# The first transfer ahead of the opening barrier, and the closing barrier with semaphores alone, in a single-core decode kernel

## The chip, the cores and the metric

The program runs on one core of one Trainium2 chip. The metric is the device time of one execution in microseconds (us). "Span" is the time from the first to the last instruction of the program in a profile; mostly about 2 us of each execution lie outside the span. Engines: PE is TensorE (PEld its weight loads), DVE is VectorE, ACT is ScalarE, POOL is GpSimd, SP is SyncE; a q after the name is the engine's sequencer. A timed run also gives its span, without a trace; a trace is one execution.

## The reference

```python
x = A_x                                            # 1 x 1 x 512, bf16
h = x + attention(layernorm(x), k_cache, v_cache, wq, wo)   # 32 query heads, 8 kv heads, 65536 keys of 128
h2 = h + ((sigmoid(g) * u) @ w_down)               # g, u: layernorm(h) @ w_gate, @ w_up; 512 -> 1792 -> 512
```

One token is decoded. The two caches are 134 MB each and are read once; the weights are 13.9 MB. There is little arithmetic per byte.

## The kernel before

Python records operations per engine and emits them with semaphores. SyncE issues every large transfer; they go to four ring slots of 4 MB.

```python
order = [("wq", 0)]                                # then K0, K1, K2, K3, K4, V0, K5, V1, ...
order += [("K", b) for b in range(NR)]
# ... cut ...
order += [("V", NB - 4), ("V", NB - 3), ("V", NB - 2), ("V", NB - 1), ("wg", 0), ("wu", 0), ("wd", 0)]
dma("act", lambda e: e.dma_start(x_row[:, :], A_x[0]), "x", name="x")
# ... cut: SyncE's transfers, each waiting until its ring slot is free; then the arithmetic ...
dma("sp", lambda e: e.dma_start(out[0].rearrange("o (g n) -> (o g) n", g=4), ...), "out", ["ysb"], "out")
op("sp", lambda e: None, ["out"])                  # SyncE waits for the output
block = es.enter_context(nc.Block("main"))         # opens one body per engine, closes with a barrier
P.emit(block)
```

The built program begins and ends with a barrier of all five engines. Each engine drains and increments a gather semaphore; GpSimd waits until it is 4, then increments a release semaphore, on which the others wait (in the trace of the opening one the gathers come at 0.01 to 0.34 us, SyncE's release at 0.66). GpSimd writes four constants before the opening one. SyncE's instructions, as built (wait in brackets):

```
opening: Drain [release == 0, then gather += 1]; EventSemaphore [release >= 1]; branch to SyncE's body
body:    DMACopy wq; DMACopy K0, K1, K2; ...; DMACopy out [y copied]; branch [output landed]
closing: Drain [release == 0, then gather += 1]; EventSemaphore [release >= 1]
```

Of the kernel before, what the change touches and what calls it, by code (L numbers as in the profile page):

```python
# [32 lines left out]
HINTED = ("pe", "dve", "act")  # L33


class Prog:
# [3 lines left out]
    def __init__(self, nc, es):  # L40
        self.nc, self.es = nc, es
        self.ops = {e: [] for e in ("pe", "act", "dve", "pool", "sp")}
        self.where = {}
        self.alias = {}
        self.dma_sems = {}
        self.loop_sems = {}
        self.flow = {}
        self.part = {}

    def op(self, eng, fn, deps=(), name=None, to=None, times=1):  # L50
        assert name is None or name not in self.where, name
        self.ops[eng].append(dict(fn=fn, deps=[d for d in deps if d], name=name, dma=None, to=to, times=times, part=self.part.get(eng)))
        if name:
            self.where[name] = (eng, len(self.ops[eng]) - 1)
# [4 lines left out]
        rec["count"] += 16  # L59
        self.ops[eng][-1]["dma"] = (sem, rec["count"])  # L60

    def emit(self, block):
        for ops in self.ops.values():
            for o in ops:
                o["deps"] = [self.alias.get(d, d) for d in o["deps"]]
        needed = {d for ops in self.ops.values() for o in ops for d in o["deps"]}
        sems = {e: self.es.enter_context(self.nc.semaphore(f"s_{e}")) for e in self.ops}
        for k, rec in self.dma_sems.items():
            rec["sem"] = self.es.enter_context(self.nc.semaphore(f"d_{k}"))
        extra = {k: self.es.enter_context(self.nc.semaphore(f"p_{k}"))  # L70
                 for k in sorted({o["to"] for ops in self.ops.values() for o in ops if o["to"]})}
        parts = {}
        for e in self.flow:
            byname = {}
            for o in self.ops[e]:
                if o["part"]:
                    byname.setdefault(o["part"][0], {}).setdefault(o["part"][1], []).append(o)
            parts[e] = byname
            for inst in byname.values():
                for same in zip(*inst.values(), strict=True):  # L80
                    assert len({o["to"] for o in same}) == 1
                    if any(o["name"] in needed for o in same):
                        for o in same:
                            o["inc"] = True
        value = {}
        counts = {}
        for e, ops in self.ops.items():
            n = 0
            for o in ops:
                if o["dma"]:  # L90
                    k, v = o["dma"]
                    value[o["name"]] = (self.dma_sems[k]["sem"], v, k)
                elif o["to"]:
                    k = o["to"]
                    counts[k] = counts.get(k, 0) + 1
                    if o["name"]:
                        value[o["name"]] = (extra[k], counts[k], k)
                    o["inc"] = True
                elif o["name"] in needed or o.get("inc"):
                    n += o["times"]  # L100
                    value[o["name"] or id(o)] = (sems[e], n, e)
                    o["inc"] = True

        def waits_of(e, o, seen, off, loop):
            want = {}
            for d in o["deps"]:
                sem, v, key = value[d]
                own = self.loop_sems.get(key, (None,))[0]
                assert own in (None, e) and not (loop and own is None), (o["name"], d)
                v -= off.get(key, 0)  # L110
                if v > seen.get(key, 0) and v > want.get(key, (None, 0))[1]:
                    want[key] = (sem, v)
            for key, (sem, v) in want.items():
                seen[key] = v
            return list(want.values())

        def put(e, eng, o, waits):
            for sem, v in waits:
                eng.wait_ge(sem, v)
            ins = o["fn"](eng)  # L120
            if o["dma"]:
                ins.then_inc(self.dma_sems[o["dma"][0]]["sem"], 16)
            elif o["to"]:
                ins.then_inc(extra[o["to"]], 1)
            elif o.get("inc"):
                ins.then_inc(sems[e], 1)

        def run(e, eng):
            ops = self.ops[e]
            if e not in self.flow:  # L130
                seen = {}
                for o in ops:
                    put(e, eng, o, waits_of(e, o, seen, {}, False))
                return
            at = [i for i, o in enumerate(ops) if o["part"]]
            head, tail = ops[:at[0]], ops[at[-1] + 1:]
            assert at == list(range(at[0], at[-1] + 1))
            seen = {}
            for o in head:
                put(e, eng, o, waits_of(e, o, seen, {}, False))  # L140
            off, plan, took, seq = {}, {}, {}, []
            for o in ops[at[0]:at[-1] + 1]:
                if not seq or seq[-1] != o["part"]:
                    seq.append(o["part"])
            assert len(set(seq)) == len(seq)
            for p, r in seq:
                s2 = {}
                w = [waits_of(e, o, s2, off, len(parts[e][p]) > 1) for o in parts[e][p][r]]
                assert plan.setdefault(p, w) == w, (p, r, plan[p], w)
                for k, v in s2.items():  # L150
                    took[k] = max(took.get(k, 0), v)
                for k, (own, down) in self.loop_sems.items():
                    if own == e and p in down:
                        assert took[k] >= down[p], (k, p, r)
                        took[k] -= down[p]
                        off[k] = off.get(k, 0) + down[p]

            done = set()

            def section(p):  # L160
                assert p not in done
                done.add(p)
                inst = list(parts[e][p].values())[-1]
                for o, w in zip(inst, plan[p]):
                    put(e, eng, o, w)
                for k, (own, down) in self.loop_sems.items():
                    if own == e and p in down:
                        eng.sem_inc(extra[k] if k in extra else self.dma_sems[k]["sem"], -down[p])

            self.flow[e](eng, section)  # L170
            assert done == set(parts[e])
            seen = {k: v for k, v in seen.items() if k not in self.loop_sems}
            for o in tail:
                put(e, eng, o, waits_of(e, o, seen, off, False))

        def hinted(e, eng):

            if self.ops[e][0]["dma"]:
                put(e, eng, self.ops[e].pop(0), [])
            here = OrderedEngineSet([eng.engine])  # L180
            never = self.nc.alloc_registers(f"never_{e}", engines=here)
            first, end = f"first_{e}", f"end_{e}"
            self.nc.regs_mov(never, 1)
            self.nc.br(first, engines=here)
            with self.nc.body(first, valid_engines=here):
                loc = eng.mark_branch_hint_location()
                run(e, eng)
                eng.br_lt(never, 1, on_true=first, on_false=end).branch_hint(loc)
            self.nc.switch_bb(end)

        for e, deco in (("sp", block.sync), ("pool", block.gpsimd), ("act", block.scalar),
                        ("dve", block.vector), ("pe", block.tensor)):
            deco((lambda eng, e=e: hinted(e, eng)) if e in HINTED else (lambda eng, e=e: run(e, eng)))


def bass_sequential_preLN__gqa_block_cached__glu_gated_glu__decode_kernel(
# [18 lines left out]
    with ExitStack() as es:  # L215
# [69 lines left out]
        P = Prog(nc, es)  # L285
        op, dma = P.op, P.dma
# [29 lines left out]
        for ld in order:  # L316
# [3 lines left out]
            deps = [freed(prev[ld])]  # L320
# [103 lines left out]
        regs, R, here = [], {}, OrderedEngineSet([mybir.EngineType.PE])  # L424
# [323 lines left out]
        for i in range(HKV + 1):  # L748
            loop = 0 < i < HKV
            for r in range(NR):  # L750
# [7 lines left out]
                if i:  # L758
                    v = NR * (i - 1) + r
# [32 lines left out]
        for i, (nm, bank) in enumerate((("wg", GB), ("wu", UB))):  # L792
            at = slot_of[(nm, 0)] * SLOT + W_AT[nm]
# [19 lines left out]
        for i, (r0, r1) in enumerate(WD_SPLIT):  # L813
            for r in range(r0, r1):
                for g in range(4):
# [5 lines left out]
        op("dve", lambda e: e.tensor_copy(y_sb[:, :], ps(YB, 0, 128)), ["y"], "ysb")  # L821
        dma("sp", lambda e: e.dma_start(out[0].rearrange("o (g n) -> (o g) n", g=4),
                                        bass.AP(tensor=y_sb, offset=0, ap=[[32 * 128, 4], [1, 128]])), "out", ["ysb"], "out")
        op("sp", lambda e: None, ["out"])

        block = es.enter_context(nc.Block("main"))
        P.emit(block)


# [26 lines left out]
```

## Time and profile before

| | before |
|---|---|
| median of the first 3 runs | 663.49 us |
| span of the profiled run | 660.9 us |
| bytes moved, mean rate | 282.3 MB, 427 GB/s |
| wq issued, first packet (records of the trace) | 0.737, 1.744 us |
| output semaphore full, SyncE's signal to the closing barrier, last release ended | 660.453, 660.643, 660.850 us |

From the page of the kernel before: the span, the busy share of the 16 DMA engines in 40 equal slices (9 is 90% or more), the rate of each slice, and the share of one queue.

```profile
span 660.9 us, 6130 instructions
...
DMA  9999999999999999999999999999999999999997
GB/s 381 440 418 438 434 426 440 420 438 434 424 440 424 434 438 420 440 424 436 436 420 440 432 428 438 420 438 434 426 440 419 438 434 426 440 422 421 435 421 320
...
q1 hardware_dynamic: 11208, 282.33, 99.5%
```

The transfers fill the time; only the first and the last slice are low. So the time is a head before the first byte, a stream, and a tail after it.

The start in the timeline of the kernel before (start, duration, engine, line, operation, what ended the idle time before it):

```profile
0.73 0.51 ACTq L312 DMA_DIRECT2D x_row<-in_A_x_dram  x1
0.74 0.39 SPq L322 DMA_DIRECT2D ring<-in_A_wq_dram  x1
...
1.19 1.46 SPq L345 DMA_DIRECT2D ring<-in_A_k_cache_dram  x3
...
2.04 0.29 PE L402 MATMUL PS<-ident,x_row 1*128 1x1 bf16 x4 [2.04 <-DMA x_row<-in_A_x_dram]
...
7.59 0.30 DVE L408 TENSOR_SCALAR xz<-hT,mo,rstd 128x4 bf16<-128x4 f32 x1 [0.68 <-POOL rstd L396]
...
13.31 0.58 PE L445 MATMUL PS<-qz 128*8 128x512 bf16 x1 [7.17 <-issue]
```

SyncE stands in the barrier for 0.7 us before it issues wq. The normalised x (xz) is ready at 7.9 us, and PE goes on only at 13.3, when wq has landed.

The end, in the same view:

```profile
656.57 0.65 DVE L812 STREAM_TRANSPOSE hhT<-hh 128x448 bf16<-128x448 bf16 x1
...
657.27 1.14 PE L817 MATMUL PS<-ring,hhT 128*1 128x128 bf16 x56 [1.71 <-DVE hhT L812]
658.12 0.10 PEld L817 LDWEIGHTS PS<-ring,hhT 128*1 128x1 bf16 x8 [0.20 <-DMA ring<-in_B_w_down_dram]
658.46 0.29 DVE L821 CAST y_sb<-PS 128x128 bf16<-128x128 f32 x1 [1.24 <-PE PS L817]
658.77 0.66 SPq L822 DMA_DIRECT2D out_dram<-y_sb  x1
```

And SyncE's waits that the change touches (engine and line, for what, total us, times, longest): the branch L215 for the output, the opening barrier L841, the closing barrier L215.

```profile
SPq L215 <- DMA out_dram<-y_sb: 1.0, 1, 1.0
SPq L841 <- PEq L841: 0.7, 1, 0.7
SPq L215 <- PEq L215: 0.2, 1, 0.2
```

### The profile page before, as it was taken

The numbers are of one execution on the slowest core, as the hardware profiler recorded it, in microseconds if no ns is written. First come the engines' busy times: TensorE is split into PE (matmuls) and PEld (weight loads), VectorE is DVE, ScalarE is ACT, GpSimd is POOL, SyncE is SP. The second block draws the span as 40 slices with busy tenths as digits, with TensorE's granted clock in tenths as the row PEclk, the third lists the DMA queues.
The fourth block names the chain that finished last, engine by engine and source line by source line (L and its number), as shares of the span: only waits on it lengthen the run. The fifth ranks groups of instructions, "written<-read, shape, count | busy, mean of one in ns | idle before, by whom it ended". The sixth has DMA issues, their size and how long they took to land. (4 is left out here: it accounts for less than half of the span.)

```text
span 660.9 us, 6130 instructions
## 1 busy us (share of the span) xinstructions
PE 424.1 (64%) x2316; PEld 73.6 (11%) x1548; DVE 350.5 (53%) x446; ACT 41.8 (6%) x111; POOL 3.6 (1%) x17
## 2 busy tenths in 40 slices
PE   2797587548666585666765485764856668555855
PEld 1100010011000010010100110001100101001322
DVE  3598755547437655346555374465743565553102
ACT  0100200020000200020000200002000110002000
POOL 1000000000000000000000000000000000000000
PEclk9899687677888697886966778766878758678576
DMA  9999999999999999999999999999999999999997
GB/s 381 440 418 438 434 426 440 420 438 434 424 440 424 434 438 420 440 424 436 436 420 440 432 428 438 420 438 434 426 440 419 438 434 426 440 422 421 435 421 320
DMA packets 11211, 282.34 MB, mean 427 GB/s; under 512 B 1225, under 2 KB 1226, under 8 KB 2250
## 3 DMA queue, kind: packets, MB, share of 16 engines
q1 hardware_dynamic: 11208, 282.33, 99.5%
q14 instruction: 1, 0.01, 0.0%
q10 hardware_dynamic: 2, 0.00, 0.0%
HBM read 282.33 MB, written 0.00 MB: 427 GB/s over the span
## 5 line engine op out<-in xcount | busy, mean ns | idle before, releaser
L419 PE MATMUL PS<-ktw 128*128 128x512 bf16 x1024 | 304.2, 447 | 160.2 <-DVE ktw L500 156.5
L500 DVE STREAM_TRANSPOSE ktw<-ring 128x1024 f32<-128x1024 f32 x256 | 291.8, 1206 | 135.9 <-DMA ring<-in_A_k_cache_dram 135.8
L419 PE MATMUL PS<-ring,PT_sb 128*32 x1024 | 83.6, 456 | 23.7 <-issue 15.9
L419 PEld LDWEIGHTS PS<-ktw 128*128 x256 | 27.3, 107 | 415.1 <-issue 260.5
L554 DVE STREAM_TRANSPOSE PT_sb<-P_sb 128x512 bf16<-128x512 bf16 x32 | 20.1, 684 | 53.7 <-PE PS L591 52.2
L540 ACT ACTIVATE negmax<-PS 128x1 f32<-128x1 f32 x8 | 1.4, 171 | 527.2 <-PE PS L538 527.2
L419 PEld LDWEIGHTS PS<-ring,PT_sb 128*32 x1024 | 25.8, 116 | 79.5 <-issue 74.2
L505 DVE TENSOR_REDUCE M_sb<-PS 128x1 f32<-128x512 f32 x32 | 19.9, 682 | 25.1 <-PE PS L419 25.1
L544 ACT ACTIVATE P_sb<-PS,negmax 128x512 bf16<-128x512 f32 x32 | 21.5, 685 | 0.3
L561 DVE TENSOR_REDUCE lsum<-PS 128x1 f32<-128x4 f32 x8 | 1.3, 161 | 30.8 <-PE PS L559 30.8
L531 PE MATMUL PS<-identf,gm 128*1 128x128 f32 x16 | 3.1, 272 | 16.9 <-DVE gm L529 16.9
L604 DVE TENSOR_TENSOR Lw<-O,blk_of 128x128 bf16<-128x128 bf16 x4 | 1.1, 282 | 20.1 <-ACT O L595 20.1
L588 ACT ACTIVATE po_sb<-PS,rl 128x512 bf16<-128x512 f32 x8 | 5.5, 687 | 54.8 <-PE PS L419 54.8
L466 DVE STREAM_TRANSPOSE qt<-qh 32x512 bf16<-32x512 bf16 x1 | 0.7, 699 | 15.3 <-ACT qh L463 15.3
L419 PE MATMUL PS<-ring,xz 128*8 x32 | 8.6, 437 | 0.0
L419 PE MATMUL PS<-ktw,O 128*1 x26 | 8.5, 505 | 0.0
L538 PE MATMUL PS<-one_f,gmrep 1*128 1x1 f32 x16 | 3.8, 307 | 5.0 <-DVE gmrep L535 5.0
L544 ACT ACTIVATION_READ_ACCUMULATOR P_sb<-PS,negmax 128x1 f32 x32 | 6.5, 203 | 0.0
L591 PE MATMUL PS<-sel_bf,po_sb 128*128 128x4 bf16 x32 | 2.1, 169 | 6.3 <-ACT po_sb L588 6.3
L647 DVE TENSOR_TENSOR yr<-PS,x_row 1x512 f32<-1x512 f32 x1 | 0.7, 679 | 9.5 <-PE PS L645 9.5
L445 PE MATMUL PS<-qz 128*8 128x512 bf16 x2 | 1.0, 482 | 7.2 <-issue 7.2
L481 ACT ACTIVATE PS<-zcol 128x512 f32<-128x512 bf16 x8 | 5.0, 622 | 0.0
(81 smaller groups left out, 69.0 us busy)
## 6 DMA issues: line engine op xcount, KB each, us to landing
ring<-in_A_k_cache_dram SPq DMA_DIRECT2D x32, 4096.0 KB, 29.5
ring<-in_A_v_cache_dram SPq DMA_DIRECT2D x31, 4096.0 KB, 27.4
ring<-in_A_wq_dram SPq DMA_DIRECT2D x1, 4096.0 KB, 12.5
ring<-in_A_v_cache_dram SPq DMA_DIRECT2D x1, 3072.0 KB, 13.0
ktw<-in_A_wo_dram SPq DMA_DIRECT2D x1, 2048.0 KB, 9.9
ring<-in_B_w_gate_dram SPq DMA_DIRECT2D x1, 1792.0 KB, 18.5
ring<-in_B_w_up_dram SPq DMA_DIRECT2D x1, 1344.0 KB, 21.1
ktw<-in_A_wo_dram SPq DMA_DIRECT2D x1, 1024.0 KB, 12.0
```

The lines of the kernel that those rows point to most:

```text
L419: return e.add_instruction(mybir.InstMatmult(name=nc.get_next_instruction_name(), engine=mybir.EngineType.PE, ins=[rhs, lhsT], outs=[e.low ...
L481: op("act", lambda e: e.activation(ps(PO, 0, 512), bass.AP(tensor=zcol, offset=0, ap=[[1, 128], [0, 512]]), AF.Copy), ["zcol"] if h == 0 e ...
L500: op("dve", lambda e, d=dst, sr=src: e.transpose(d, sr), deps, f"T{b}.{c}", to="T")
L505: op("dve", lambda e, u=u: e.tensor_reduce(M_sb[:, u % 4:u % 4 + 1], ps(u % NS, 0, 512), AX.X, ALU.max), [f"S{b}.{NC - NR + k}"], f"mx{u}" ...
L531: op("pe", lambda e: e.matmul(ps(MISC, 0, 128, 0, 1), lhsT=gm[:, :], rhs=identf[:, :], start=True, stop=True), [f"gm{h}"], f"gmT{h}", to="Q")
L538: op("pe", lambda e: e.matmul(ps(MISC, 128, 129), lhsT=gmrep[0:1, :], rhs=one_f[0:1, 0:1], start=True, stop=True), [f"gmrep{h}"], f"neg{h}")
L540: op("act", lambda e: e.activation(negmax[:, k:k + 1], ps(MISC, 128, 129), AF.Copy, scale=-att_scale), [f"neg{h}"], f"negmax{h}")
L544: op("act", lambda e, b=b: e.activation(P_sb[:, (b % 4) * 512:(b % 4 + 1) * 512], ps(b % NS, 0, 512), AF.Exp, bias=negmax[:, k:k + 1], sca ...
L554: op("dve", lambda e, b=b: e.transpose(PT_sb[:, (b % 4) * 512:(b % 4 + 1) * 512], P_sb[:, (b % 4) * 512:(b % 4 + 1) * 512]), [f"E{b}", f"o ...
L561: op("dve", lambda e: e.tensor_reduce(lsum[:, :], ps(MISC, 132, 136), AX.X, ALU.add), [f"l{h}"], f"ls{h}", to="D")
L588: op("act", lambda e: e.activation(po_sb[:, :], ps(PO, 0, 512), AF.Copy, scale=rl[:, :]), [f"PV{NR * h + NR - 1}", f"rl{h}"], f"po{h}", to ...
L591: op("pe", lambda e, t=t: e.matmul(ps(OX, 0, 4), lhsT=po_sb[:, t * 128:(t + 1) * 128], rhs=sel_bf[:, 8 * t:8 * t + 8:2], start=(t == 0), s ...
```

## The change

The first transfer needs nothing from the barrier: nothing else touches its slot. So it moves ahead of SyncE's drain. At the end SyncE branches to the closing block first and waits there, in the barrier's own instruction; the closing barrier uses semaphores without drains.

```diff
-    def emit(self, block):
+    def emit(self):
 ...
-        for e, deco in (("sp", block.sync), ("pool", block.gpsimd), ("act", block.scalar), ...):
-            deco((lambda eng, e=e: hinted(e, eng)) if e in HINTED else (lambda eng, e=e: run(e, eng)))
+        nc, entry = self.nc, self.nc.cur_bb.bb
+        first = self.ops["sp"].pop(0)
 ...
+        put("sp", nc.sync, first, [])
+        code = list(entry.instructions)
+        load = code.pop()
+        at = [i for i, ins in enumerate(code) if isinstance(ins, mybir.InstDrain) and ins.engine == mybir.EngineType.SP]
+        code.insert(at[0], load)
+        entry.instructions = code
 ...
+        for e, eng in (("sp", nc.sync), ("pool", nc.gpsimd), ...):
+            here = OrderedEngineSet([eng.engine])
+            nc.br(f"prog_{e}", engines=here)
+            with nc.body(f"prog_{e}", valid_engines=here):
+                (hinted if e in HINTED else run)(e, eng)
+                nc.br("fin", engines=here)
+        nc.switch_bb("fin")
+        for sem, v, _ in (value[d] for d in self.at_end):
+            nc.sync.wait_ge(sem, v)
+        nc.all_engine_barrier(sem_only=True)
 ...
-        op("sp", lambda e: None, ["out"])
-        block = es.enter_context(nc.Block("main"))
-        P.emit(block)
+        P.at_end = ("out",)
+        P.emit()
```

The order of all other instructions on each engine is unchanged, the barriers and branches apart.

More of the change, by code (lines that the diff above doesn't have):

```diff
@@ L48, in __init__ @@
         self.part = {}
+        self.at_end = ()
     def op(self, eng, fn, deps=(), name=None, to=None, times=1):
@@ L65, in emit @@
                 o["deps"] = [self.alias.get(d, d) for d in o["deps"]]
-        needed = {d for ops in self.ops.values() for o in ops for d in o["deps"]}
+        needed = {d for ops in self.ops.values() for o in ops for d in o["deps"]} | set(self.at_end)
         sems = {e: self.es.enter_context(self.nc.semaphore(f"s_{e}")) for e in self.ops}
@@ L189, in hinted @@
             self.nc.switch_bb(end)
-        for e, deco in (("sp", block.sync), ("pool", block.gpsimd), ("act", block.scalar),
-                        ("dve", block.vector), ("pe", block.tensor)):
-            deco((lambda eng, e=e: hinted(e, eng)) if e in HINTED else (lambda eng, e=e: run(e, eng)))
+        nc, entry = self.nc, self.nc.cur_bb.bb
+        first = self.ops["sp"].pop(0)
+        assert first["dma"] and not first["deps"]
+        put("sp", nc.sync, first, [])
[4 more added lines that the diff above has]
+        entry.instructions = code
+        entry = nc.cur_bb
+        for e, eng in (("sp", nc.sync), ("pool", nc.gpsimd), ("act", nc.scalar), ("dve", nc.vector), ("pe", nc.tensor)):
+            here = OrderedEngineSet([eng.engine])
[7 more added lines that the diff above has]
+        nc.all_engine_barrier(sem_only=True)
 def bass_sequential_preLN__gqa_block_cached__glu_gated_glu__decode_kernel(
```

## The prediction

> **What bounds the kernel now.** The page shows the 16 DMA engines at 9 tenths in 39 of 40 slices, queue 1 with 99.5% of their span, 282.3 MB at 427 GB/s. A 4 MB cache transfer lands 27 to 30 us after its issue, though the first K transfers land 9.7 us apart: two or three are always queued, so SyncE's waits for buffers do not starve the stream. The packet records run without a gap from 1.74 to 657.66 us. So the time is head + fixed stream + tail.
>
> **Head.** SyncE's first record is its drain of the opening barrier at 0.00. GpSimd sets the barrier (four constants, then its event at 0.53); SyncE is released at 0.66 and issues wq at 0.737 (timeline). The first packet comes 1.0 us later. Issued ahead of the drain, wq should start at about 0.00, its first packet at 1.0, and every landing come 0.74 us earlier. The issue takes 0.39 us; SyncE then reaches the barrier at about 0.45, before GpSimd's 0.53, so the barrier ends within 0.1 us of where it did, and the next K issue (1.19 before) comes at about 0.75.
>
> Side effect: x (1 KB, ScalarE's queue, still after the barrier) had its packet at 1.62, just before the stream. Now wq's 32 KB packets, about 2 us each, are ahead. [...] so x should land some us after its 1.99. No cost: the copy that uses it waits for VectorE's constants until 4.96, and xz is ready at 7.89 against wq at 13.2 us.
>
> **Middle.** Same instructions in the same order on each engine. K3 needs wq's slot, freed at about 22.4 us; K1 and K2 are queued then. No change.
>
> **Tail.** The last values wait for the last V piece (landed 645.01); then 13 us of small steps run beside the last weights, whose last piece lands at 658.08 and releases the last 8 matmuls. Both shift with the stream, so the 0.74 us survive. The output's semaphore is full at 660.45; SyncE's waiting branch runs at 660.47, its drain only at 660.63, its signal at 660.64, then GpSimd and the release, end 660.85. With the wait in the barrier's own instruction the branch is taken while the output is in flight; the signal comes at about 660.49: 0.15 us saved. The drains are worth little: SyncE's took 13 ns [...], the others' ended earlier. Nearly all of the end's saving is the branch, not "semaphores alone".
>
> **Sum.** 0.74 + 0.15 = 0.89 us of 663.49, all on the critical path: 662.6 us; range 662.1 to 663.1, as runs spread by 0.56 us. Chances: faster by over 2% 0.005, within 2% 0.985, slower by over 2% 0.01.
>
> **Right or wrong in the profile.** wq's issue at 0.0 to 0.1 us in the timeline; its landing near 12.5 instead of 13.2; last wd about 0.7 us earlier from the start; the closing branch's wait on the output gone from SyncE's waits, one on the barrier instruction in its place; span about 660.0; x later than 1.99.
>
> **What would make it wrong.** SyncE's drain waits for the transfer's descriptors and holds up the barrier; something outside the program's records (fetches end at -0.06 us) holds the early transfer; x lands after 9 us; the tail's chain doesn't shift with the stream; or the span's zero moves and time outside the span (1.8 us in the profiled run) grows.

Two passages are cut from the prediction where marked, as no trace of this case shows them: a rule on when x's packet gets its turn, and a figure for drains beside the 13 ns of the trace. They hold no term of the sum: 0.74 us (head) and 0.15 us (closing), 0.89 us in all, from 663.49 to 662.6. That x would land "some us" later rested on the first of them: it was the author's estimate.

## The result

| | before | changed |
|---|---|---|
| median, first comparison (6 and 6 runs) | 663.33 us | 662.03 us (661.85 to 662.98) |
| median, second comparison (9 and 5 runs) | 663.34 us | 662.34 us (661.97 to 663.50) |
| ratio, first | | 0.9983 (95%: 0.9970 to 0.9996) |
| ratio, second | | 0.9991 (95%: 0.9977 to 1.0004) |

A ratio is the mean time of one kernel's fast runs over that of the other's of the same rounds, so it is not quite the ratio of the medians. By these figures the change saves between 0.6 and 1.3 us, but the intervals are wide: the first reaches from 0.3 to 2.0 us, and the second includes no saving at all. "Within 2%" is the class.

From the page of the changed kernel, the same lines:

```profile
span 659.8 us, 6128 instructions
...
DMA  9999999999999999999999999999999999999997
GB/s 397 429 445 419 439 429 429 443 417 443 425 433 441 417 445 419 439 429 429 443 417 443 429 429 441 417 445 423 435 429 429 443 419 441 429 429 419 439 418 329
...
q1 hardware_dynamic: 11208, 282.33, 99.7%
```

The same bytes at the same rate in a shorter span. The start of the changed kernel in the timeline:

```profile
0.00 0.39 SPq L341 DMA_DIRECT2D ring<-in_A_wq_dram  x1
...
0.80 0.51 ACTq L331 DMA_DIRECT2D x_row<-in_A_x_dram  x1
0.81 1.36 SPq L364 DMA_DIRECT2D ring<-in_A_k_cache_dram  x3
...
7.22 0.29 PE L421 MATMUL PS<-ident,x_row 1*128 1x1 bf16 x4 [7.22 <-DMA x_row<-in_A_x_dram]
...
10.19 0.30 DVE L427 TENSOR_SCALAR xz<-hT,mo,rstd 128x4 bf16<-128x4 f32 x1 [0.68 <-POOL rstd L415]
...
12.28 0.58 PE L464 MATMUL PS<-qz 128*8 128x512 bf16 x1 [3.54 <-issue]
```

wq is issued at 0.00 and PE begins 1.03 us earlier. x now lands behind wq's packets, 5.2 us later, and still in time: xz is ready at 10.5. The end:

```profile
656.43 1.05 PE L836 MATMUL PS<-ring,hhT 128*1 128x128 bf16 x56 [1.70 <-DVE hhT L831]
657.53 0.29 DVE L840 CAST y_sb<-PS 128x128 bf16<-128x128 f32 x1 [1.16 <-PE PS L836]
657.85 0.65 SPq L841 DMA_DIRECT2D out_dram<-y_sb  x1
```

And SyncE's waits. The wait for the output now stands at L212, the barrier itself:

```profile
SPq L212 <- DMA out_dram<-y_sb: 1.0, 1, 1.0
SPq L212 <- PEq L212: 0.2, 1, 0.2
SPq L858 <- PEq L858: 0.2, 1, 0.2
```

The records (instruction starts, packet starts, semaphore increments) place the difference of the two spans, 1.10 us: the first packet comes at 1.02 instead of 1.74 (0.72); the closing, from the full output semaphore to SyncE's signal, takes 0.02 instead of 0.19 (0.17); 0.2 us more went somewhere between. That remainder is what the first experiments were for. The zero of the span, which the prediction named as a risk, did not move: GpSimd writes its first constant at 0.24 us before and 0.23 after, and the time outside the span stayed at about 2 us.

### The profile page after: what moved, and what is told of

The parts are those of the page before. It is cut to its first block, busy times and chain, and to the rows that moved or that the text cites. A ratio compares the mean times of both kernels' runs of the same rounds, so it can differ in the third digit from the quotient of the medians.

```text
span 659.8 us, 6128 instructions
## 1 busy us (share of the span) xinstructions
PE 419.5 (64%) x2316; PEld 72.6 (11%) x1548; DVE 350.5 (53%) x446; ACT 41.8 (6%) x111; POOL 3.6 (1%) x17
## 5 line engine op out<-in xcount | busy, mean ns | idle before, releaser
L438 PE MATMUL PS<-ktw 128*128 128x512 bf16 x1024 | 300.9, 442 | 163.9 <-DVE ktw L519 160.2
L438 PE MATMUL PS<-ktw,O 128*1 x26 | 6.9, 431 | 0.0
```

Of the source, the lines that this page charges most:

```text
L438: return e.add_instruction(mybir.InstMatmult(name=nc.get_next_instruction_name(), engine=mybir.EngineType.PE, ins=[rhs, lhsT], outs=[e.low ...
```

## The experiments

Theories. A: the head and the closing add up, and x's packet, which went just ahead of the stream before, made a DMA engine lag (wq's 128 packets of 32 KB ran 16 at a time, the page counts 16 DMA engines, and wq's landing counted its semaphore up 16 times, which I take as one landing for each engine; in the first trace of before, these 16 landings were spread over 0.90 us, in that of the changed kernel over 0.51), so moving it gave the rest. B: the rest is chance. C: the closing does most. Later, D: the rest is where the windows of TensorE's granted clock fall in the last steps, by chance (in the traces of before and of the changed kernel the granted clock changes between 0.50 and 1.00, and every recorded stretch of one clock but the last lasts 3.41 us or a whole multiple of it); E: the new ending saves something more.

All twelve experiments gave the right result; before_again, after_again and tail_again repeat a kernel. Edits are against the changed kernel where no other is named. The kernel before ran on the same chip in the same rounds, 9 times for each group of four in the table; its mean spans were 661.22, 661.28 and 661.19 us.

| kernel | mean span (5 runs) | under before | ratio of times |
|---|---|---|---|
| head_alone | 660.54 | 0.68 | 0.9992 (0.9978 to 1.0005) |
| tail_alone | 660.76 | 0.46 | 0.9992 (0.9978 to 1.0006) |
| x_late | 661.20 | 0.02 | 0.9997 (0.9983 to 1.0010) |
| x_early | 660.34 | 0.88 | 0.9990 (0.9976 to 1.0003) |
| after_again | 660.32 | 0.96 | 0.9991 (0.9977 to 1.0004) |
| tail_again | 660.76 | 0.52 | 0.9996 (0.9982 to 1.0010) |
| sem_alone | 660.38 | 0.90 | 0.9986 (0.9972 to 0.9999) |
| wait_alone | 660.22 | 1.06 | 0.9989 (0.9976 to 1.0003) |
| wq_late | 663.64 | -2.45 | 1.0031 (1.0018 to 1.0045) |
| four_early | 660.06 | 1.13 | 0.9981 (0.9967 to 0.9994) |
| no_closing | 659.82 | 1.37 | 0.9971 (0.9957 to 0.9984) |
| before_again | 661.10 | 0.09 | 0.9999 (0.9986 to 1.0013) |

The spans of five runs of one kernel lie up to 0.6 us on either side of their mean, and the intervals of the ratios are about 0.9 us wide on each side. So the timed runs can't tell 0.2 us apart; the verdicts below rest on the records of the traces, where one step is seen to some hundredths. They are:

```
              wq      first   wq's 16 landings    x       last V   chain to  output   signal
              issued  packet  last    spread      landed  piece    y's copy  full     after it
before        0.74    1.74    13.22   0.90        1.99    645.01   13.45     660.45   0.190
after         0.00    1.02    12.19   0.51        7.17    644.10   13.43     659.52   0.024
head_alone    0.00    1.04    12.36   0.61        7.03    644.28   14.16     660.43   0.190
tail_alone    0.73    1.76    12.99   0.49        2.38    644.80   13.75     660.55   0.023
x_late        0.74    1.75    13.09   0.70        7.83    644.92   14.13     661.04   0.190
x_early       0.00    1.01    12.20   0.49        1.80    644.15   14.09     660.24   0.024
after_again   0.00    1.02    12.26   0.55        7.23    644.21   13.43     659.64   0.023
tail_again    0.74    1.76    12.98   0.63        1.99    644.90   13.43     660.32   0.023
sem_alone     0.00    1.02    12.28   0.48        7.19    644.19   13.82     660.01   0.196
wait_alone    0.00    1.04    12.12   0.37        6.88    643.98   13.73     659.71   0.120
wq_late       3.13    4.14    15.42   0.62        1.96    647.33   14.15     663.48   0.190
four_early    0.00    1.03    12.53   0.83        8.14    644.30   13.49     659.79   0.023
no_closing    0.00    1.02    12.24   0.49        7.06    644.03   13.75     659.77   -
before_again  0.74    1.76    13.00   0.56        2.35    644.97   13.72     660.69   0.190
```

"Chain to y's copy" is the time from the landing of the last V piece to the start of the copy of y: the last values, the output projection, the norm and the feed-forward part. From that copy to the full output semaphore it is 1.99 to 2.00 us in every trace.

### head_alone

```diff
-        P.at_end = ("out",)
+        op("sp", lambda e: None, ["out"])
-        nc.all_engine_barrier(sem_only=True)
+        nc.all_engine_barrier()
```

> The early wq transfer with the old ending (SyncE waits for the output before its branch, barrier with drains). Theory A (head, engine skew and tail add up): wq issued at 0.00, first packet near 1.02, last DMA engine's share of wq landed near 12.2 us, the last weights near 657.15; from the full output semaphore to SyncE's signal 0.19 us as in the kernel before; span 659.9, about 0.95 us under the kernel before. Theory B (only the 0.72 us of the head carry over, the rest of what the changed kernel gained in the stream was chance of that run): the last weights near 657.35, span 660.1. Rival C (the closing does most of it): span within 0.2 us of the kernel before.

The head did what was expected (first packet 1.04, signal after 0.190, mean span 0.68 us under before), but the trace ended at 660.82, not at 659.9. The last weights had landed at 657.34, in time; the copy of y began 1.1 us after that. The timeline at the end of head_alone:

```profile
656.72 1.66 PE L836 MATMUL PS<-ring,hhT 128*1 128x128 bf16 x56 [1.70 <-DVE hhT L831]
658.44 0.29 DVE L840 CAST y_sb<-PS 128x128 bf16<-128x128 f32 x1 [1.77 <-PE PS L836]
```

The same 56 matmuls took 1.05 us in the changed kernel's trace and 1.66 here. The windows view gives the reason; its columns are the stretch, its length, busy time of each engine, the granted TensorE clock, the DMA share and GB/s. The changed kernel:

```profile
core 0: us, PE busy (x) PEld busy (x) DVE busy (x) ACT busy (x) POOL busy (x), PEclk, DMA share, GB/s
645.00:649.00 4.00, 1.82 (x22) 0.77 (x23) 0.46 (x2) 0.86 (x2) 0.00 (x0) 0.50 1.00 422
656.50:658.50 2.00, 0.98 (x56) 0.68 (x56) 0.29 (x1) 0.00 (x0) 0.00 (x0) 0.84 0.02 6
```

head_alone:

```profile
645.00:649.00 4.00, 1.74 (x21) 0.57 (x18) 0.45 (x2) 0.86 (x2) 0.00 (x0) 0.83 0.98 413
656.50:658.50 2.00, 1.66 (x56) 1.37 (x56) 0.23 (x2) 0.00 (x0) 0.00 (x0) 0.50 0.03 10
```

In head_alone the full clock fell on 646 to 650 and the last matmuls had half; in the changed kernel's trace it was the other way round. So single spans can't be compared without the chain's length, and theory D was formed here.

### tail_alone

```diff
-        first = self.ops["sp"].pop(0)
-        # ... and the lines that move it ahead of the drain
```

> The new ending with wq behind the barrier. All theories but C: wq issued at 0.73 to 0.74, first packet at 1.74; from the full output semaphore to SyncE's signal 0.03 us instead of 0.19; span 0.16 us under the kernel before, 660.7, too little to see in the timed runs. Rival C: most of the 1.1 us is here, span near 660.0.

The signal came 0.023 us after the full semaphore, as expected. The mean span lay 0.46 us under before, not 0.16. C is out, since head_alone has 0.68 without the new closing; but the surplus of 0.3 needed a second look (tail_again).

### x_late

Against the kernel before:

```diff
-        dma("act", lambda e: e.dma_start(x_row[:, :], A_x[0]), "x", name="x")
+        dma("act", lambda e: e.dma_start(x_row[:, :], A_x[0]), "x", ["xz0"], "x")
-                put(e, eng, self.ops[e].pop(0), [])
+                o = self.ops[e].pop(0)
+                put(e, eng, o, waits_of(e, o, {}, {}, False))
```

> The kernel before with x's 1 KB transfer issued about 0.6 us later (after GpSimd's second memset), so that its packet comes behind the first wq packets. Theory A says that the x packet ahead of the stream makes a DMA engine lag for the whole execution: spread of the 16 landings of wq falls from 0.90 to about 0.5 us, the last one at 12.8 to 12.9 instead of 13.22, and the last weights land near 657.7 instead of 658.08; span 660.5. Theory B (the lag is chance or comes from something else): spread and landing as in the kernel before, 0.8 to 0.9 us and 13.2 us. Both: x lands several us later, near 7 us.

x went behind the stream (landed 7.83), but the last of wq's landings came at 13.09, the spread was 0.70, and the mean span stayed. Neither A's nor B's number was hit; x_early decides.

### x_early

```diff
+        put("act", nc.scalar, self.ops["act"].pop(0), [])
+        # ... moved ahead of ScalarE's drain, in the way of wq
```

> The changed kernel with x's transfer also ahead of the barrier, so that x and wq stand to one another as in the kernel before. Theory A: x lands near 1.4 us, the spread of wq's 16 landings goes up from 0.51 to about 0.9 us, the last one lands near 12.5 instead of 12.19, and the last weights 0.3 us later than in the changed kernel; span 660.1. Theory B: spread as in the changed kernel, 0.5 us, span 659.8. Both: the earlier x does not make anything faster.

x landed at 1.80, ahead again, and the spread stayed at 0.49, the last landing at 12.20. In before_again x was ahead as well, with a spread of 0.56. Theory A falls: where x's packet goes doesn't set the spread, which ranges from 0.37 to 0.90 over the fourteen traces with no order that I can see. What sets it stays open. The mean span, 0.88 us under before, is that of the changed kernel too; the single trace was longer (660.5) because its chain was 14.09.

### after_again

> The changed kernel once more, beside the kernel before on this chip. Theory D (head 0.72 us + closing 0.17 us = 0.89 us; what the first comparison showed beyond that was where the throttle's full-clock window happened to fall in the last small steps): mean span 0.9 us under the kernel before, between 0.7 and 1.1, and the chain from the last V piece to the copy of y takes 13.4 us where the window of full clock covers the last matmuls and 14.1 us where it doesn't. Theory E (a third saving of 0.2 to 0.3 us exists): 1.1 to 1.2 us again.

0.96 us under before: D's range held (0.7 to 1.1). The window of full clock covered the last matmuls again, and the chain took 13.43 us as expected.

### tail_again

> The new ending alone a second time; its first mean span lay 0.46 us under the kernel before where its records of the closing account for 0.17. Theory D: 0.1 to 0.3 us now. Theory E (the new ending saves something besides the closing): 0.4 to 0.5 us again.

0.52 us again: E's number, not D's. No record shows where the whole surplus over 0.17 is. Up to the last V piece it is 0.07 to 0.11 us ahead of the kernel before's two traces, and its chain, with full clock at the end, is as long as that of before with full clock at the end (13.43 and 13.45). An estimate from the traces: span minus chain is 647.31 to 647.41 us in before, before_again and x_late, and 647.04 and 647.13 in tail_alone and tail_again, so about 0.3 us of the 0.5 lie outside the chain (0.17 of them the closing), and the other 0.2 would be that the five runs happened to have shorter chains. That is not shown, as the timed runs have no traces.

### sem_alone

```diff
-        P.at_end = ("out",)
+        op("sp", lambda e: None, ["out"])
```

> The changed kernel, but SyncE waits for the output before its branch again; the closing barrier still uses semaphores alone. If the branch is the saving, as predicted: from the full output semaphore to SyncE's signal 0.17 to 0.19 us, as in the kernel before, and no more than 0.02 us is left of the closing's saving. If the drains are the saving: 0.03 us, as in the changed kernel. Mean span 0.7 us under the kernel before.

The signal took 0.196 us: leaving the drains out alone saved nothing. The branch's record began at 660.025, the next instruction at 660.186: 0.16 us for the way into the closing block, now after the output (in the kernel before 660.469 and 660.629, of which the branch's own record takes 33 ns).

### wait_alone

```diff
-        nc.all_engine_barrier(sem_only=True)
+        nc.all_engine_barrier()
```

> The changed kernel with the wait after the branch, but drains in the closing barrier. The wait is then an instruction of its own before SyncE's drain. If the branch is the saving: from the full output semaphore to SyncE's signal 0.04 to 0.08 us (the wait and a drain of 13 ns, with an issue between). If the drains are the saving: 0.15 us or more. Mean span 0.85 us under the kernel before.

0.120 us, between the two expectations. With drains the builder gives the wait an instruction of its own: the wait ran at 659.723, the drain at 659.812 (13 ns long), the signal after it. So of the 0.17 us of the closing, 0.07 came with the branch's move and 0.10 more when the drain fell away and the wait went into the barrier's own instruction, which of the two barriers built here only the one without drains allowed. The two halves of the edit don't add up singly: 0 and 0.07 alone, 0.17 together.

### wq_late

Against the kernel before:

```diff
-            deps = [freed(prev[ld])]
+            deps = [freed(prev[ld])] + (["Wz"] if k == "wq" else [])
```

> The kernel before with wq's issue held until GpSimd's last memset of the start (about 3.1 us instead of 0.74), so the stream starts about 2.4 us later. If the head lies on the critical path one to one, as predicted: first packet near 4.15, last weights near 660.4, mean span 2.4 us over the kernel before (2.2 to 2.6). If the stream or the tail has slack that takes up part of a shift of the head: clearly under 2.2.

From the timeline of wq_late:

```profile
0.73 0.51 ACTq L312 DMA_DIRECT2D x_row<-in_A_x_dram  x1
...
3.13 0.39 SPq L322 DMA_DIRECT2D ring<-in_A_wq_dram  x1
```

The issue came 2.39 us later, the last V piece 2.41 us later than the mean of the five traces with wq's issue at 0.74 (644.92), and the mean span rose by 2.45 us. The shift runs through one to one, as expected; the whole middle has no slack to take it up.

### four_early

```diff
+        for _ in range(4):
             first = self.ops["sp"].pop(0)
             # ... the same lines, once for each of wq, K0, K1, K2
```

> The changed kernel with the first three K transfers ahead of the barrier too. SyncE comes to the barrier at about 1.9 us and every engine is released at about 2.0 instead of 0.72. If only the first transfer's issue matters and the barrier is off the critical path: x lands near 8.4, xz is ready near 11.7, still ahead of wq at 12.2, and the span is that of the changed kernel, 660.2 within 0.2. If the barrier's own end matters: up to 1.3 us more, 661.5.

From the timeline of four_early:

```profile
0.00 0.39 SPq L342 DMA_DIRECT2D ring<-in_A_wq_dram  x1
0.44 1.47 SPq L365 DMA_DIRECT2D ring<-in_A_k_cache_dram  x3
...
2.32 0.50 ACTq L332 DMA_DIRECT2D x_row<-in_A_x_dram  x1
...
11.15 0.30 DVE L428 TENSOR_SCALAR xz<-hT,mo,rstd 128x4 bf16<-128x4 f32 x1 [0.68 <-POOL rstd L416]
```

The barrier released the engines at 2.24 instead of 0.72, and the mean span was 660.06, within 0.2 of the expected 660.2. Within that noise the barrier as such costs nothing (after_again had 660.32); what counts is that the first transfer stood behind it. xz was ready 1.1 us ahead of wq, so there is no room for much more.

### no_closing

```diff
-        nc.all_engine_barrier(sem_only=True)
```

> The changed kernel without a closing barrier: SyncE alone waits for the output, the other engines end. The records between SyncE's signal and the last engine's release, 0.21 us, fall away: span 0.2 us under the changed kernel, 660.0. If time outside the program follows SyncE's end, the timed runs fall by the same 0.2 us; if what comes after waits for something else, they stay. Result correct in any case, as SyncE waits for the output.

The mean span was 1.37 us under before, and the timed runs fell further: median 661.45, mean 661.44 against 663.36 of before, 1.92 us. So more than the 0.21 us of the records is gone. Other records show where: semaphore 2, which no instruction of the program waits for or updates, is updated 18 times after the last release (661.09 to 662.77 us in the kernel before, 659.98 to 661.67 in the changed kernel). What updates it was not shown. In this trace four of its updates came at 657.9 to 658.2, while the output was still under way, where the changed kernel has all of them after its last release. From the full output semaphore to the last such update it took 1.51 us here, 2.15 in the changed kernel, 2.32 in the kernel before, and between 2.14 and 2.53 in all thirteen traces with a closing barrier.

This is the fastest version, clear of noise against the kernel before. It wasn't run in the same rounds as the changed kernel; each against before, the medians differ by 1.93 and 1.00 to 1.30 us. The nearest kernel of the same rounds is four_early, which differs from the changed kernel by the early K transfers alone: its mean span is 0.24 us longer than no_closing's, its mean time 0.87 us (662.31). So some 0.6 us were saved outside the span, which fits the difference of 1.51 and 2.14 or more in the records. SyncE still waits for the output before it ends, and the five runs were right. Whether such an ending is as safe in a program of several cores was not tried.

### before_again

> The kernel before against itself: the difference of the two mean spans is the noise of such a comparison. Theory D (the new ending's extra 0.3 us is the throttle's windows falling differently by chance): up to 0.3 us, and the trace, if its last matmuls fall in a half-clock window, ends later than the first trace of this kernel by 0.5 to 0.7 us, all of it in the chain from the last V piece to the copy of y (14.1 instead of 13.45 us). Theory E: under 0.1 us, and the chain the same length in any window.

0.09 us between the two means of the same kernel, which D (up to 0.3) and E (under 0.1) both allow; but the chain, which E held to be of one length, was not. The last matmuls had half clock this time (0.50 over 656.5 to 658.5, where the first trace had 1.00):

```profile
656.97 1.66 PE L817 MATMUL PS<-ring,hhT 128*1 128x128 bf16 x56 [1.69 <-DVE hhT L812]
658.69 0.29 DVE L821 CAST y_sb<-PS 128x128 bf16<-128x128 f32 x1 [1.77 <-PE PS L817]
```

They took 1.66 instead of 1.14 us, but the chain was 13.72, not the 14.1 that I expected, because a second window of full clock (645.88 to 649.30; 0.89 granted over 645 to 649, against 0.50 in the first trace) shortened the last values. Over the fourteen traces the chain has three lengths. It takes 13.43 to 13.49 us when a window of full clock covers the last matmuls or most of them (before, after, after_again, tail_again, four_early); 13.72 to 13.82 when the last window begins 0.9 to 1.4 us after the last V piece has landed, so that it covers part of the last values (before_again, tail_alone, sem_alone, wait_alone, no_closing); 14.09 to 14.16 when it begins 1.9 to 2.1 us after that landing, or when there is none (head_alone, x_late, x_early; wq_late). That the chain's length goes with the window, in the same kernel too, is shown; that this is all of tail_alone's surplus is not. The shortest length has another limit: in every trace the last weights land 13.04 to 13.08 us after the last V piece, and in the five traces with the short chain the last 8 matmuls begin within 0.05 us of that.

## Why the prediction was right, and where it was not

- Bound by the stream, time = head + stream + tail: right, and shown by wq_late, where a shift of 2.39 us came out as 2.45, and four_early, where the barrier itself moved by 1.5 us at no cost that the spans show.
- Head, 0.74 us: right. The first packet came 0.72 us earlier (1.01 to 1.05 us after the start of wq's issue in all fourteen traces). Over all traces the last V piece landed at 644.92 on average with wq's issue at 0.74 (5 traces) and at 644.16 with wq's issue at 0.00 (8 traces): 0.76 us. wq's last landing moved from 13.06 to 12.27 on average, against 13.2 and 12.5 in the prediction.
- SyncE at the barrier at 0.45, before GpSimd's 0.53: the step failed, without cost. SyncE's drain began at 0.45 but took 0.12 us after the transfer's issue (0.01 before), so its signal came at 0.58 and set the barrier: release at 0.72 instead of 0.66. The next K issue came at 0.81 instead of 0.75.
- x "some us" late: right, it landed at 7.17; the margin before wq shrank from 5.3 to 1.7 us. "About 2 us each" holds for the first 16 of wq's packets alone (median 1.95 us in the changed kernel's trace); the later ones of wq took 1.21. And x paid twice: its 1 KB packet started at 5.60, 4.8 us after its issue (0.9 in the kernel before), the next packet of its queue, of 4 bytes, at 6.85, 1.25 us later, about the time of one of wq's packets, and only then did it land.
- Closing, 0.15 us: right in size (0.17 in the records). Wrong in its split: "Nearly all of the end's saving is the branch, not 'semaphores alone'". The branch alone gave 0.07 us, the barrier without drains alone nothing, both 0.17. SyncE's closing drain is short, as stated (13 ns in the kernel before), but a barrier with drains keeps the wait in a separate instruction (0.09 us ahead of the drain in wait_alone).
- Tail: the shift survived, as predicted. "The last piece lands at 658.08 and releases the last 8 matmuls" was true of the one trace read; in all others but four_early those weights were there before the PE came to them (by 0.05 to 0.6 us), and the chain of small steps ended last. Its length varies by 0.7 us between executions, as much as the head's gain. That was missing from "what would make it wrong", and it is the spread of the runs that the range should have come from. So whether a median of five or six runs falls inside a range of 1 us is in part luck.
- Sum: 0.89 predicted. Records: 0.76 + 0.17 = 0.93. Timed: 1.13 us and 0.60 us by the two ratios, 1.30 and 1.00 by the medians. The first median, 662.03, lies 0.07 under the range's low end of 662.1; the second, 662.34, inside it.
- Open: the new ending alone lay 0.46 and 0.52 us under before in two sets of five runs, of which its records account for 0.17; and what sets the spread of the 16 landings, which an execution keeps in the main (0.90 us at wq and 0.81 at the last V piece in the kernel before, 0.51 and 0.52 in the changed kernel).

## What to carry to other kernels

Here transfers filled the whole time, and what came before the first byte counted in full (2.39 us came out as 2.45 in wq_late, 0.74 as 0.76 at the last V piece). In such a kernel issue the first transfer ahead of everything that it does not need, and check only that small loads that now queue behind it still come in time (x came 5.2 us later, and 1.7 us were left). At the end, take the way to the last wait (branches, separate instructions) while the last write is in flight, so that the wait itself is the signal (0.17 us here); and ask whether the closing barrier is needed at all (without it the median lay 1.93 us under before, with it 1.00 to 1.30). For gains under 1 us, compare landmarks in the records over several traces: a single span here moved by 0.7 us with the clock (chain of 13.43 to 14.16 us), and the means of five times lie within intervals of about 0.9 us on each side.
